# A chunked attention with two MoE layers: 64x64 score and value products, the first unit's products among them, and the third pair's operands built in place

## The chip, the cores and the metric

One core of a Trainium2 chip runs the program in one launch. The metric is device time in microseconds (us). An execution is about 2 us longer than the span of its profile, which goes from the first to the last instruction. Engines are called as in the profile: PE (matrix products), PEld (their weight loads), DVE (vector), ACT (scalar), POOL (GpSimd), SP (the queue that issues DMAs).

## What is computed

```python
def _attn_ref(q, k, v):                      # 4 batches, 8 heads, 576 x 64, chunks of 64
    scores = scale * np.matmul(q_c, k_c.transpose(0, 1, 2, 4, 3))
    scores = scores - np.max(scores, axis=-1, keepdims=True)
    attn = np.exp(scores)
    attn = attn / (np.sum(attn, axis=-1, keepdims=True) + 1e-09)
    out = np.matmul(attn, v_c)

def _moe_ref(x, w_in, w_out, s, b):          # 2304 tokens, 512 -> 2048 -> 512
    h = x @ w_in
    r = np.maximum(h, 0.0)
    g = s * (r * r) + b
    return g @ w_out

def _moe2_ref(x, w_gate, w1, w2):            # 8 experts, 512 -> 1024 -> 512
    P = np.exp(logits - logits.max())        # logits = x @ w_gate
    for _ in range(8):
        P /= P.sum(1, keepdims=True) + 1e-09
        P /= P.sum(0, keepdims=True) + 1e-09
        P *= N / E
    for e in range(E):
        out += P[:, e:e + 1] * (np.maximum(x @ w1[e], 0.0) @ w2[e])
```

Attention runs inside chunks of 64 tokens: for each chunk and head a 64x64 score matrix and a 64x64 by 64x64 value product. Its output, transposed, is the x of the first MoE layer, and that layer's output the x of the second.

## The kernel before

**Attention** goes over 18 tiles of 128 tokens (two chunks each, 8 heads in 4 pairs). `attn_stages(t)` is a generator of five stages: 0 transposes q and k on PE (`pq`, `pk`) and evicts them by ACT; 1 the scores (`sc`) with row maximum and subtraction on DVE; 2 exponential (ACT), sums and reciprocals (DVE), scaling (POOL); 3 the transpose of the probabilities (`pa`); 4 the value product (`px`), whose eviction makes the high part `xTh` (ACT) and the low part `xTl` (DVE). Both products run over all 128 partitions with zeros beside the blocks: k is evicted into the block-diagonal `kbd` (lines 259 to 263), v is loaded into the block-diagonal `vbd` (line 131), and both tiles are filled with zeros at the start (lines 888 to 891). `attention()` sets the order of the stages of the tiles, one tile entering per round.

**The first MoE layer** takes every fp32 product as three products of high and low parts (`three`, line 107). Its 2048 hidden columns are eight units of 256. For each unit `u` and each group `g` of three tiles there is `up1` (two banks `ph` of 12 products each, then relu, square, scale and the split into `gh`, `gl`) and `down1` (four banks `po` of 6). In the main loop `down1` of a group is called after `up1` of the next one (`prev`). In unit 0 the attention stages are called between the products by `stage`. The weights come as 64-bit numbers and are converted by `convert` and `finish` on ACT, DVE and POOL; `next(cg)` takes one step of that.

**The second MoE layer** multiplies 2x2 blocks by Winograd's variant of Strassen's scheme: three pairs of groups, `build_x(p)` makes the seven operands of pair `p` from the blocks a11, a12, a21, a22, each as a high part (ACT, line 519) and a low part (DVE, line 520), with sums (DVE, line 523) into scratch tiles. `up_chain(n, p)` is a chain of seven products of six matmuls; its banks come from a cycle, its evictions are `s11`, `s12` (line 665), `s22` (line 669), `s21` (674 to 677). Lines 686, 688 and 691 are copies by ACT that the chain's own later products need. `order` lists the chains; `advance` takes steps of the generators in `work` between products (preparing weight blocks `prep_w1`, building x). `prep_w1(n + 2)` is started when weight block `n` has had its last use. `prep_w2_first` makes the first operands of the down chains (line 714 the split's high part, 715 the low part, 718 the subtraction). Each `down_chain` takes four banks from `kept["abc"]`, the fourth being the target of its second product.

What sets the order on each engine is the order in which the code calls these generators: every engine works through its own instructions in program order and waits on semaphores.

## Time and profile before

| | before |
|---|---|
| median of 3 runs | 1969.03 us (1967.58 to 1971.49) |
| the profiled execution | 1969.52 us, span 1967.7 us |
| PE / PEld | busy 98% / 97% of the span |
| DVE / ACT / POOL | busy 70% / 50% / 8% |
| DMA queue 1 | 333.5 MB, 52.2% of 16 engines' span |
| granted PE clock, mean | 0.996 |

The span divides into attention with unit 0 (to 150 us), units 1 to 7 of the first layer (to about 519 us), the up chains of the second layer (to about 1235 us) and its down chains. A busy PE is not a PE at its peak, since matmuls are pipelined and their ends are modelled; durations of one matmul overlap those of the next, so spacing is read from one row's start to the next row's start. `x16` in a row of the timeline means sixteen instructions merged; a number in brackets is the idle time ahead of it and what ended that.

### The profile page before, as it was taken

What the parts mean: (1) busy time and instruction counts of PE and PEld (TensorE: products, weight loads), DVE (VectorE), ACT (ScalarE), POOL (GpSimd) and SP (SyncE); (2) the same over time, 40 slices, a digit from 0 to 9 for tenths busy, and PEclk for the clock granted to TensorE, in tenths of its full rate; (3) what the DMA queues carried; (4) which work ended last, traced back from release to release, by engine and by line L of the source; (5) the groups of instructions that cost most, each with busy time, mean ns of one, the idle gap of its engine ahead of it and who ended that gap; (6) DMA issues with size and microseconds to landing.
All of it is one profiled execution on the core that took longest, in us unless ns stands there. A gap on an engine that the chain in (4) does not pass through costs nothing.

```text
span 1967.7 us, 33548 instructions
## 1 busy us (share of the span) xinstructions
PE 1933.7 (98%) x13283; PEld 1911.3 (97%) x13283; DVE 1374.4 (70%) x2365; ACT 993.6 (50%) x1793; POOL 158.1 (8%) x128
## 2 busy tenths in 40 slices
PE   7999999999899999999999999999999999999999
PEld 6899999999799999999999999999999999999998
DVE  5656777775767666656565656888887878788775
ACT  5664333335544445444444444555555555555553
POOL 4333333330000000000000000000000000000000
PEclk9999999999999999999999999999999999999999
DMA  8521111100155565556555656867676766767675
GB/s 201 133 65 44 44 43 43 43 22 11 39 201 213 196 228 219 208 202 227 218 210 202 225 218 232 287 184 225 177 229 188 223 201 208 220 190 227 180 228 167
DMA packets 295726, 335.64 MB, mean 171 GB/s; under 512 B 65937, under 2 KB 254353, under 8 KB 295569
## 3 DMA queue, kind: packets, MB, share of 16 engines
q1 hardware_dynamic: 295568, 333.50, 52.2%
q8 instruction: 104, 1.70, 0.3%
q14 instruction: 54, 0.43, 0.1%
HBM read 196.63 MB, written 136.84 MB: 169 GB/s over the span
## 4 chain that ended last, share of the span: by engine, by line
PE 92%; ACT 3%; DVE 3%; issue 1%; POOL 0%; DMA 0%; SPq 0%; DVEq 0%; ACTq 0%; POOLq 0%
PE wb L611 71%; PE po L107 10%; PE ph L107 9%; PE px L303 1%; PE sc L272 1%; ACT kbd L261 0%; ACT whole L659 0%; PE pa L295 0%; DVE x L520 0%; ACT r L368 0%; DMA raw<-in_moe_w_in_dram 0%; ACT r L358 0%; DVE sm L287 0%; DVE xs L523 0%; ACT qT L254 0%
## 5 line engine op out<-in xcount | busy, mean ns | idle before, releaser
L611 PE MATMUL wb<-x,x 128*128 128x256 f32 x6048 | 727.2, 283 | 2.3 <-DVE whole L665 1.4
L611 PEld LDWEIGHTS wb<-x,x 128*128 128x128 f32 x6048 | 726.3, 192 | 3.2 <-DVE whole L665 1.6
L611 PE MATMUL wb<-x,w1h 128*128 128x384 f32 x2688 | 687.8, 337 | 6.9 <-ACT wb L686 3.2
L611 PEld LDWEIGHTS wb<-x,w1h 128*128 128x128 f32 x2688 | 485.5, 188 | 9.8 <-ACT wb L686 4.2
L611 PE MATMUL wb<-x,w1l 128*128 128x384 f32 x1344 | 452.3, 337 | 0.1
L816 DVE TENSOR_TENSOR x<-st,x 128x1024 fp32r<-128x1024 f32 (+1 forms) x288 | 308.0, 1088 | 101.5 <-ACT x L815 100.5
L815 ACT ACTIVATE x<-st 128x1024 fp32r<-128x1024 f32 (+1 forms) x288 | 272.1, 945 | 109.6 <-issue 74.4
L611 PEld LDWEIGHTS wb<-x,w1l 128*128 128x128 f32 x1344 | 253.2, 188 | 0.4 <-DVE w1l L573 0.4
L843 DVE SCALAR_TENSOR_TENSOR whole<-wb,lg,whole 128x256 f32<-128x256 f32 (+1 forms) x333 | 165.9, 529 | 49.7 <-PE wb L611 47.2
L849 ACT ACTIVATE wb<-wb 128x256 f32<-128x256 f32 x216 | 79.4, 368 | 232.3 <-PE wb L611 221.7
L674 DVE SCALAR_TENSOR_TENSOR whole<-wb,whole 128x384 f32<-128x384 f32 x192 | 98.0, 552 | 126.9 <-PE wb L611 105.5
L659 ACT ACTIVATE whole<-whole 128x384 f32<-128x384 f32 x192 | 100.3, 527 | 157.1 <-DVE whole L665 119.4
L107 PE MATMUL po<-gh,wh 128*128 128x384 f32 x384 | 130.1, 339 | 0.0
L107 PE MATMUL ph<-xTh,wh 128*128 128x384 f32 x384 | 129.0, 336 | 0.7 <-ACT xTh L311 0.7
L107 PE MATMUL ph<-xTl,wh 128*128 128x384 f32 x384 | 128.4, 334 | 0.3 <-DVE xTl L312 0.3
L107 PE MATMUL po<-gh,wl 128*128 128x384 f32 x384 | 128.4, 334 | 0.0
L107 PE MATMUL po<-gl,wh 128*128 128x384 f32 x384 | 128.4, 334 | 0.0
L107 PE MATMUL ph<-xTh,wl 128*128 128x384 f32 x384 | 128.3, 334 | 0.0
L360 DVE SCALAR_TENSOR_TENSOR r<-r,s_bc 128x384 f32<-128x384 f32 x84 | 65.9, 785 | 70.7 <-ACT r L358 70.7
L573 DVE TENSOR_TENSOR w1l<-w,w1h 128x512 fp32r<-128x512 f32 (+1 forms) x128 | 78.9, 619 | 34.3 <-ACT w1h L571 34.3
L691 ACT ACTIVATE whole<-wb 128x384 f32<-128x384 f32 x96 | 47.4, 494 | 93.9 <-PE wb L611 93.8
L364 ACT ACTIVATE gh<-r,b_bc 128x384 fp32r<-128x384 f32 x84 | 51.8, 617 | 84.3 <-DVE r L360 84.3
(135 smaller groups left out, 2022.9 us busy)
## 6 DMA issues: line engine op xcount, KB each, us to landing
h<-whole SPq DMA_DIRECT2D x96, 1344.0 KB, 5.0
st<-h SPq DMA_DIRECT2D x216, 512.0 KB, 4.2
w<-in_moe_w_dram SPq DMA_DIRECT2D x60, 512.0 KB, 6.8
st<-h SPq DMA_DIRECT2D x72, 256.0 KB, 4.2
raw<-in_moe_w_in_dram SPq DMA_DIRECT2D x16, 512.0 KB, 3.7
raw<-in_moe_w_out_dram SPq DMA_DIRECT2D x14, 512.0 KB, 3.5
vbd<-in_v_dram SPq DMA_DIRECT2D x72, 64.0 KB, 2.5
out_dram<-whole SPq DMA_DIRECT2D x18, 256.0 KB, 3.3
```

Source lines behind the costliest of these rows:

```text
L107: nc.tensor.matmul(out, lhsT=x, rhs=y, start=(i == 0), stop=(i == n - 1))
L360: nc.vector.scalar_tensor_tensor(out=r, in0=r, scalar=s_bc[:, 0:1], in1=r, op0=ALU.mult, op1=ALU.mult)
L364: nc.scalar.activation(out=hh, in_=r, func=AF.Identity, bias=b_bc[:, 0:1])
L573: nc.vector.tensor_tensor(out=dst(lo), in0=src, in1=dst(hi).bitcast(F32), op=ALU.subtract)
L611: nc.tensor.matmul(out, lhsT=x, rhs=y, start=fresh and i == 0, stop=i == n - 1, skip_group_check=True)
L659: nc.scalar.activation(out=dst, in_=src, func=AF.Relu)
L674: nc.vector.scalar_tensor_tensor(out=dst, in0=view(b), scalar=0.0, in1=y, op0=ALU.max, op1=op)
L691: nc.scalar.activation(out=u2, in_=b, func=AF.Copy)
L815: nc.scalar.activation(out=h, in_=src, func=AF.Copy)
L816: nc.vector.tensor_tensor(out=l, in0=src, in1=h.bitcast(F32), op=ALU.subtract)
L843: nc.vector.scalar_tensor_tensor(out=dst, in0=src, scalar=g, in1=dst, op0=ALU.mult, op1=ALU.add)
L849: nc.scalar.activation(out=dst, in_=src, func=AF.Copy)
```

## The change

The diff has six parts.

1. **Scores and values on 64x64 blocks.** `kbd` and `vbd` go, with their zero fills. k is evicted whole into `kT` by one activation. Each head and chunk has its own product with 64 rows and 64 columns of the array; a tile's scores lie in two banks and its values in two, and the row maximum, the subtraction and the two evictions of the values are done per bank. For the second chunk the two heads of a pair change places (`head`). v is loaded three tiles ahead instead of two.
2. **First loads.** q and k of tile 1 and v of tile 0 are issued ahead of the first weight block; the conversions begin at later stages.
3. **Unit 0.** `down1` of a group follows `up1` of the same group, with attention stages dealt between the products by a list.
4. **The third pair's operands** are built in place, in another order, at listed places of the first chains; the chains (0, 2) and (1, 1) change places, and the logits of the last group are made in the first chain.
5. **`prep_w2_first`** makes operand 2 ahead of operand 1.
6. **The down chains' fourth bank** is 7 and 6 in place of 6 and 7.

```diff
@@ attention
-    kbd = [cv.tile([P, NP, 2, 2, CH], F32, ...), ...]
-    vbd = [cv.tile([P, NP, 2, 2, D], F32, name=f"vbd{i}") for i in range(2)]
+    vs = [cv.tile([P, NP, 2, D], F32, name=f"vs{i}") for i in range(3)]
+    def head(s, c):
+        return s if c == 0 else 1 - s
...
-        for j in range(2):
-            h = slice(j * D, (j + 1) * D)
-            nc.scalar.activation(
-                out=kb[h, :, :, j, :],
-                in_=pk[h].rearrange("x (p c t) -> x p c t", p=NP, c=2), func=AF.Copy,
-            )
+        kT = at.tile([P, NP, P], F32, tag="kT", name=f"kT{t}")
+        nc.scalar.activation(out=kT.rearrange("x p t -> x (p t)"), in_=pk, func=AF.Copy)
...
+        sc = [bank(f"sc{t}_{s}")[:, :NP * CH] for s in range(2)]
         for p in range(NP):
-            for c in range(2):
-                nc.tensor.matmul(
-                    sc[c * CH:(c + 1) * CH, p * P:(p + 1) * P],
-                    lhsT=qT[:, p, c * CH:(c + 1) * CH],
-                    rhs=kb[:, p, c].rearrange("x j t -> x (j t)"),
+            for s in range(2):
+                for c in range(2):
+                    h = slice(head(s, c) * D, (head(s, c) + 1) * D)
+                    k = slice(c * CH, (c + 1) * CH)
+                    nc.tensor.matmul(
+                        sc[s][k, p * CH:(p + 1) * CH], lhsT=qT[h, p, k], rhs=kT[h, p, k],
...
+        for s in range(2):
+            sc3 = sc[s].rearrange("t (p k) -> t p k", p=NP)
+            nc.vector.tensor_reduce(out=mx[:, s], in_=sc3, axis=AX.X, op=ALU.max)
+            nc.vector.tensor_tensor(
+                out=pr[:, s::2], in0=sc3, in1=mx[:, s].to_broadcast([P, NP, CH]), op=ALU.subtract)
...
+        px = [bank(f"px{t}_{c}")[:, :NP * CH] for c in range(2)]
         for p in range(NP):
             for c in range(2):
+                for s in range(2):
+                    r = slice(s * CH, (s + 1) * CH)
+                    nc.tensor.matmul(
+                        px[c][head(s, c) * D:(head(s, c) + 1) * D, p * CH:(p + 1) * CH],
+                        lhsT=vb[r, p, c, :], rhs=aT[r, p, c * CH:(c + 1) * CH],
@@ build_x, third pair only
+        if p == NPR - 1:
+            split(0, a11)
+            yield
+            split(6, a22)
+            combine(a22, a21, a22, ALU.add)
+            yield
+            split(1, a22)
+            combine(a21, a21, a11, ALU.subtract)
+            yield
+            combine(a11, a22, a11, ALU.subtract)
+            split(2, a11)
+            yield
+            split(3, a12)
+            combine(a12, a12, a11, ALU.subtract)
+            yield
+            split(4, a12)
+            yield
+            split(5, a21)
+            yield
+            return
@@ down_banks, prep_w2_first
-        kept["abc"] = itertools.cycle([(0, 2, 5, 6), (1, 3, 4, 7)])
+        kept["abc"] = itertools.cycle([(0, 2, 5, 7), (1, 3, 4, 6)])
...
-            w2_split(0, 1, b22, f)
-            yield
             w2_split(0, 2, b11, f)
             w2_combine(b21, b21, b11)
+            yield
+            w2_split(0, 1, b22, f)
@@ main loop, unit 0
-            if i in (0,2,4,7,10,13,16,18):
+            if i in (4, 7, 8, 10, 11, 13):
                 next(cg, None)
...
+                if u == 0:
+                    steps = iter((2, 1, 0, 2, 2, 2, 2, 1))
+                    def side():
+                        stage(next(steps, 2))
+                        if g == 0:
+                            next(cg, None)
+                hs = up1(u, g, side)
+                if u == 0 and g < NG - 1:
+                    stage(next(steps))
+                    later()
+                    stage(next(steps))
+                    down1(u, g, hs, side)
...
@@ up chains
-        order = [(0, 0), (0, 1), (1, 0), (1, 1), (0, 2), (1, 2)] + ...
+        order = [(0, 0), (0, 1), (1, 0), (0, 2), (1, 1), (1, 2)] + ...
-        work += [prep_w1(1), build_x(2), next_weights(2)]
+        work += [prep_w1(1), next_weights(2)]
+        third = build_x(2)
...
-                advance(3 if i == 5 else 2 if i == 0 or left in (4, 5) else 1)
+                if (i, s) in ((0, 3), (1, 0), (1, 2), (2, 0), (2, 1), (2, 3), (3, 0)):
+                    next(third)
+                if i == 0:
+                    for _ in range((2, 1, 9, 0)[s]):
+                        next(lgen, None)
+                advance(2 if i == 5 or left in (4, 5) else 1)
```

Three places show what moves. On SP's queue, the first loads of the program; before:

```order
L120 DMA q_112<-in_q_dram 128x8x64
L120 DMA k_113<-in_k_dram 128x8x64
L177 DMA raw_156<-in_moe_w_in_dram 128x4x256
L120 DMA whole<-in_q_dram 128x8x64
L120 DMA whole<-in_k_dram 128x8x64
L177 DMA raw_160<-in_moe_w_in_dram 128x4x256
L131 DMA vbd_110<-in_v_dram 64x4x64 x4
```

and after:

```order
L118 DMA q_111<-in_q_dram 128x8x64
L118 DMA k_112<-in_k_dram 128x8x64
L118 DMA q_113<-in_q_dram 128x8x64
L118 DMA k_114<-in_k_dram 128x8x64
L129 DMA vs_108<-in_v_dram 64x4x64 x4
L118 DMA whole<-in_q_dram 128x8x64
L118 DMA whole<-in_k_dram 128x8x64
L175 DMA raw_162<-in_moe_w_in_dram 128x4x256
```

The first weight block (`raw`) has moved behind q and k of tiles 1 and 2 and v of tile 0.

On PE, behind the second bank of up products of group 0; before, three rounds of attention follow and then group 1's `ph`:

```order
L107 MATMUL ph_0_1_533<-xTh_192,wl_155 128x384
L295 MATMUL pa_553<-ident,pr 128x128 x4
L252 MATMUL pq_560<-ident,whole 128x128 x4
L258 MATMUL pk_567<-ident,whole 128x128 x4
L272 MATMUL sc_582<-kbd,qT_504 64x128 x8
L295 MATMUL pa_606<-ident,whole 128x128 x4
L303 MATMUL px_613<-aT_558,vbd_111 128x64 x8
L252 MATMUL pq_628<-ident,whole 128x128 x4
```

and after, where `sc_0` and `sc_1` are the two banks of one tile (two of four such pairs of rows are shown):

```order
L269 MATMUL sc_0_634<-kT_535,qT_528 64x64 x2
L269 MATMUL sc_1_635<-kT_535,qT_528 64x64 x2
L292 MATMUL pa_661<-ident,pr_115 128x128 x4
L249 MATMUL pq_668<-ident,q_113 128x128 x4
L255 MATMUL pk_675<-ident,k_114 128x128 x4
L105 MATMUL po_0_0_684<-gh_0_0_552,wh_152 128x384
L105 MATMUL po_0_0_684<-gl_0_0_553,wh_152 128x384
L105 MATMUL po_0_0_684<-gh_0_0_552,wl_153 128x384
L105 MATMUL po_0_0_684<-gh_0_1_621,wh_152 128x384
L105 MATMUL po_0_0_684<-gl_0_1_622,wh_152 128x384
```

Group 0's down products (`po_0_0`) now stand four short steps behind its `ph`; before they stood behind the `ph` of group 1.

On DVE, between the last evictions of chain 0 (`s21`) and the first of chain 1 (`s12`, `s22`); before, where `xs` are the scratch sums and `x_1` the low parts of the third pair:

```order
L674 SCALAR_TENSOR_TENSOR whole<-wb_5306,whole 128x3x128 x2
L676 TENSOR_TENSOR whole<-whole 128x3x128
L677 TENSOR_TENSOR whole<-whole 128x3x128
L523 TENSOR_TENSOR xs_2_5381<-xs_2_5380,whole 128x768
L520 TENSOR_TENSOR x_1_5296<-xs_2_5380,x_0_5295 128x768
L523 TENSOR_TENSOR xs_2_5421<-whole,xs_2_5381 128x768
L520 TENSOR_TENSOR x_1_5296<-xs_2_5381,x_0_5295 128x768
L665 TENSOR_TENSOR whole<-wb_5310,whole 128x3x128
L669 TENSOR_TENSOR whole<-wb_5307,c_0_1_5373 128x3x128
```

and after:

```order
L694 SCALAR_TENSOR_TENSOR whole<-wb_5700,whole 128x3x128 x2
L696 TENSOR_TENSOR whole<-whole 128x3x128
L697 TENSOR_TENSOR whole<-whole 128x3x128
L593 TENSOR_TENSOR w1l_5723<-w_1_5660,w1h_5722 128x2x2x128
L519 TENSOR_TENSOR x_1_5690<-whole,x_0_5689 128x768
L522 TENSOR_TENSOR whole<-whole 128x768
L685 TENSOR_TENSOR whole<-wb_5704,whole 128x3x128
L689 TENSOR_TENSOR whole<-wb_5701,c_0_1_5777 128x3x128
```

Two of the four operations of the third pair have moved away from here, and one low part of weight block 1 has come.

## Rows read from the trace of the kernel before

**Rows 1.** Stretches: length, busy us of each engine, PEclk, DMA share, GB/s.
```profile
0.00:35.27 35.27, 23.35 (x172) 19.57 (x173) 19.43 (x36) 19.86 (x34) 18.25 (x26) 0.90 0.84 195
35.27:150.45 115.18, 110.65 (x888) 103.93 (x886) 69.83 (x130) 75.97 (x143) 36.31 (x31) 0.97 0.46 110
63.12:91.18 28.06, 27.77 (x249) 25.60 (x249) 19.26 (x37) 20.41 (x39) 9.51 (x8) 1.00 0.52 117
150.45:470.00 319.55, 319.55 (x1845) 319.55 (x1845) 221.58 (x392) 129.13 (x240) 103.54 (x72) 1.00 0.12 39
...
1220.00:1225.00 5.00, 5.00 (x22) 5.00 (x21) 3.65 (x8) 1.81 (x4) 0.00 (x0) 0.66 0.48 191
```

**Rows 2.** Timeline of PE, start: start us, duration us, instruction, idle ahead.
```profile
8.06 1.12 PE L252 MATMUL pq<-ident,whole 128*128 128x128 f32 x4 [1.84 <-DMA whole<-in_q_dram]
...
18.55 1.09 PE L295 MATMUL pa<-ident,pr 128*128 128x128 f32 x4 [2.83 <-POOL pr L290]
...
35.30 0.42 PE L107 MATMUL ph<-xTh,wh 128*128 128x384 f32 x1
```

**Rows 3.** Timeline of PE, one attention round at full clock, and group 0's logits.
```profile
79.25 0.34 PE L107 MATMUL po<-gh,wl 128*128 128x384 f32 x1
79.52 1.09 PE L272 MATMUL sc<-kbd,qT 128*64 128x128 f32 x16
80.54 0.66 PE L295 MATMUL pa<-ident,pr 128*128 128x128 f32 x4
81.03 1.90 PE L303 MATMUL px<-aT,vbd 128*128 128x64 f32 x16
82.74 0.42 PE L107 MATMUL po<-gh,wh 128*128 128x384 f32 x1
...
83.87 0.60 PE L252 MATMUL pq<-ident,whole 128*128 128x128 f32 x4
84.31 0.60 PE L258 MATMUL pk<-ident,whole 128*128 128x128 f32 x4
...
470.86 0.85 PE L409 MATMUL pl<-whole,wg 128*32 128x384 f32 x8
```

**Rows 4.** Groups by line, ACT, 35.27 to 150.45: busy us, mean ns, idle ahead.
```profile
L261 ACT ACTIVATE kbd<-pk 64x512 f32<-64x512 f32 x28 | 16.5, 588 | 0.3
...
L311 ACT ACTIVATE xTh<-px 128x512 fp32r<-128x512 f32 x15 | 8.9, 594 | 4.8 <-PE px L303 4.7
```

**Rows 5.** The page's costliest groups: an ACT copy of 128x256.
```profile
L849 ACT ACTIVATE wb<-wb 128x256 f32<-128x256 f32 x216 | 79.4, 368 | 232.3 <-PE wb L611 221.7
```

**Rows 6.** Timeline of DVE: one operation at 512 and at 256 columns.
```profile
573.91 0.68 DVE L573 TENSOR_TENSOR w1l<-w,w1h 128x512 fp32r<-128x512 f32 x1
...
576.55 0.42 DVE L573 TENSOR_TENSOR w1l<-w,w1h 128x256 fp32r<-128x256 f32 x1
```

**Rows 7.** Timeline of PE, first up product of group 1.
```profile
63.12 0.44 PE L107 MATMUL ph<-xTh,wh 128*128 128x384 f32 x1 [0.69 <-ACT xTh L311]
```

**Rows 8.** Timeline of ACT, first bank of group 0: relu and high part.
```profile
37.74 0.49 ACT L358 ACTIVATE r<-ph 128x384 f32<-128x384 f32 x1
...
38.91 0.62 ACT L364 ACTIVATE gh<-r,b_bc 128x384 fp32r<-128x384 f32 x1 [0.69 <-DVE r L360]
```

**Rows 9.** Waits of PE, 505 to 610: us in total, times, longest.
```profile
PE wb L611 <- ACT w1h L571: 2.2, 1, 2.2
...
PE wb L611 <- DVE whole L669: 1.4, 1, 1.4
PE wb L611 <- ACT wb L686: 1.1, 1, 1.1
```

**Rows 10.** Waits of PE, 1185 to 1260.
```profile
PE wb L611 <- ACT wb L686: 2.2, 2, 1.8
PE wb L611 <- DVE whole L665: 1.4, 1, 1.4
```

**Rows 11.** Timeline of ACT before the down chains: a split of `prep_w2_first`.
```profile
1218.38 0.63 ACT L714 ACTIVATE x<-whole 128x512 fp32r<-128x512 f32 x1 [1.49 <-DVE whole L718]
```

More of the change, by code (lines that the diff above doesn't have):

```diff
@@ L129, in load_v @@
             bb, s0 = divmod(t * P + c * CH, S)
-            for j in range(2):
+            for h in range(2):
                 nc.sync.dma_start(
-                    out=vbd[t % 2][j * CH:(j + 1) * CH, :, c, j, :],
+                    out=vs[t % 3][h * CH:(h + 1) * CH, :, c, :],
                     in_=v[bb, :, s0:s0 + CH, :].rearrange(
                         "(p two) s d -> two s p d", two=2
-                    )[j],
+                    )[head(h, c)],
                 )
@@ L245, in attn_stages @@
             xT[g] = new_x(g)
-        vb = vbd[t % 2]
-        kb = kbd[t % 2]
+        vb = vs[t % 3]
         a = qt.pop(t)
@@ L887, in chunk_attention_ffn_moe @@
         nc.gpsimd.memset(ones, 1.0)
-        for z in kbd:
-            nc.vector.memset(z, 0.0)
-        for z in vbd:
-            nc.gpsimd.memset(z, 0.0)
         plan_unit(0)
-        load_raw(0)
         load_qk(1)
-        load_raw(1)
         load_v(0)
         load_qk(2)
+        load_raw(0)
+        load_v(1)
+        load_raw(1)
+        load_v(2)
         load_raw(2)
         load_raw(3)
-        load_v(1)
         nc.sync.dma_start(out=s_bc, in_=s.partition_broadcast(P))
@@ L956, in chunk_attention_ffn_moe @@
                     next(cg, None)
-                hs = up1(u, g, side if u else lambda: stage(3))
-                if u == 0 and g == 0:
-                    for _ in cg:
-                        pass
-                    plan_unit(1)
-                    cg = unit_conversion(4)
-                    next(cg)
-                elif u == 0 or g:
+                if u == 0:
[10 more added lines that the diff above has]
+                    down1(u, g, hs, side)
+                    if g == 0:
+                        for _ in cg:
+                            pass
+                        plan_unit(1)
+                        cg = unit_conversion(4)
+                    else:
+                        next(cg, None)
+                    continue
+                if u == 0 or g:
                     next(cg, None)
@@ L1020, in advance @@
                         work.pop(0)
-        order = [(0, 0), (0, 1), (1, 0), (1, 1), (0, 2), (1, 2)] + [(n, p) for n in range(2, NF - 2) for p in range(NPR)]
+        order = [(0, 0), (0, 1), (1, 0), (0, 2), (1, 1), (1, 2)] + [(n, p) for n in range(2, NF - 2) for p in range(NPR)]
         order += [(NF - d, p) for d, p in ((2, 1), (2, 0), (1, 1), (2, 2), (1, 0), (1, 2))]
```

49 lines of the change are left out of this document (17 added, 32 removed).

## The prediction

> **What bounds the kernel now.** I read the profile from the outside in: busy time by stage, then TensorE's own waits, then the rows of the engines that it waited for. By stage [rows 1], PE is busy for all 319.55 us between 150.45 and 470 us, and for 23.35 of the first 35.27, 110.65 of the next 115.18; behind 470 us its waits sum to some microseconds, in the first chains of the second MoE and at the change to the down chains [rows 9, 10]. So the time is PE's work plus a few waits in three places, and an edit counts only where it shortens PE's row of work or one of those waits. The diff touches just these three places; the rest of the program keeps its instructions. No other engine is near full: in the densest part of the attention stage (63 to 91 us) DVE is busy 19.26 of 28.06 us and ACT 20.41 [rows 1].
>
> All sums are made against the profiled execution, 1969.52 us; it is 0.5 us above the median of the three runs, which is less than any step below is certain.
>
> **Attention, start (to 35.30, the first product of unit 0).** PE waits here for transfers and for tile 0's softmax: for q of tile 1 until 8.06, for POOL's scaling of tile 0 until 18.55 [rows 2]. Ahead of tile 1's q and k in SP's queue stood a weight block of 512 KB, which at the 195 GB/s of this stretch [rows 1] is 2.7 us. The new order puts q and k of tile 1 first, and the conversions of the weight blocks start four stages later, so ACT and DVE do tile 0 first. The weight blocks are then late by the transfers that pass them: for the first block q, k of tiles 1 and 2 and v of tile 0, 1.3 MB or 6.6 us; ph of group 0 needs two of them converted by then, so the cover is there but no longer wide. I take 4 us earlier; bounds 1 and 6. The removed zero fills ran while PE waited for the first q: nothing. The bursts of this stretch lie beside waits: nothing.
>
> **Attention, the products.** Count the tiles behind 35.3: kbd has 28 evictions there, so 14 tiles' scores; xTh has 15, so 15 tiles' values [rows 4]. One sc burst takes 1.02 us from its start to the next instruction (79.52 to 80.54), and the product ahead of it is followed after 0.27 instead of the usual 0.173 (319.55 us over 1845 products), so entering this array mode costs 0.10: 1.12 in all. One px burst takes 1.71 (81.03 to 82.74) [rows 1, 3]. A pass of 128 columns over the whole array takes 0.11 (four transposes in 0.44, 83.87 to 84.31). Sixteen sc passes of the same width would be 1.76 in a row; they take 1.02, since the two halves of the array work side by side: 8 x 0.109 = 0.87, and 0.15 for leaving. The logits row says so more strongly: eight passes of 384 columns on four strips of the array in 0.85, where one after the other is 8 x 0.33 = 2.6 [rows 3]. px has only 64 columns a pass but 128 of weights, and costs 0.107 a pass.
>
> After the change both bursts are 32 passes of 64 columns with 64 columns of weights, eight on each quarter of the array. A pass is then about half of 0.109, 0.055. If the four quarters run side by side a burst is 8 x 0.055 + 0.25 = 0.69: sc saves 0.43 x 14 = 6.0, px 1.02 x 15 = 15.3, together **21.3 us**. Other ends: quarters in pairs only, 16 x 0.055 + 0.25 = 1.13, sc nothing, px 0.58 x 15 = 8.7; no overlap, 32 x 0.055 + 0.25 = 2.01, a loss of 12.5 + 4.5 = 17.0. Before shows column strips side by side, and no quarter that shares its columns with another; I take the four, since halves and strips both kept their full rate.
>
> The Trainium skill, TensorEngine Tiling (Array Packing), Restrictions and Gotchas, speaks against it: row tiles write to different PSUM banks and cannot access one bank at the same time. Here each bank receives quarters of both row halves (on different partitions). By that rule a burst is the pair price. No run here shows two row tiles.
>
> ACT saves one eviction per tile (two kbd of 0.588 become one kT) and splits xTh (0.594) into two of about 0.37, the 128x256 row [rows 4, 5]; DVE's three operations per tile become halves, each 0.42 against 0.68 for the whole [rows 6], 0.16 more for a pair. All of it lies beside PE as long as neither engine fills up (third rival).
>
> **Attention, new waits.** Before, down products ran one group behind; now po of a group follows its own ph. Two places get less cover. First, px now stands directly ahead of ph of groups 1 to 3, where PE needs the evicted values. Once this happened before, at 63.12, and cost 0.69 and a little more for the low part [rows 7]; with two ACT halves in a row I take three waits of 1.5, less the one there was: 3.5 us. Second, the chain ph, r, r squared, gh, gl: r starts at 37.74, gh ends at 39.53 [rows 8], and gl adds 0.6, so 2.4 us behind ph. PE has pa, one burst, pq, pk and the five po products that come before gl is needed: 0.44 + 0.69 + 0.88 + 0.87 = 2.9 in groups 0 to 3, two px (1.4 + 0.87) in group 4. Alone that would cover it; ACT and DVE also serve the softmax, and in group 0 the last weight conversion (DVE, ACT, POOL in turn) ends there too. I take 3 us. Bounds for both together: 0 and 12.
>
> Sum to the first product of unit 1: before 150.45; 264 unit-0 products stand ahead of it in both programs, so their cost cancels. 4 + 21.3 - 6.5 = **18.8 us** earlier.
>
> **First chains of the second MoE.** PE waits 1.4 us there for DVE L669, 1.1 for ACT L686 and 2.2 for ACT's w1h [rows 9]. The first two come from the third pair's build: four DVE operations of about 0.9 stand between two chain evictions. Now two of these and a 0.6 split stand there, some 1.1 less of 1.4, and ACT's queue has one split (0.83) less ahead of L686. The 2.2 goes because chain (0, 2) moves up one place: the last use of weight block 0 is one chain (42 x 0.173 = 7.3 us) earlier, and with it the preparation of block 2. What could come late instead is the third pair itself, needed one chain sooner; its last splits are placed one product ahead of use. The logits of group 5 move from a later chain into the first, at the same price. I take **4 us**, bounds 1 and 5.
>
> **Change to the down chains.** PE waited 1.8 us for ACT L686 (of 2.2 in two) [rows 10], and ACT had itself been held 1.49 by a split that waited for DVE's subtraction L718 [rows 11]. The swap of the splits puts one there whose operand is long done. Behind that wait the granted clock fell to 0.66 over 5 us, the mean of 1.2 and 2.4 GHz stretches [rows 1], 1.7 us lost; without the wait I expect no fall. Against it: the moved split returns one step later with DVE full. The other wait, 1.4 for DVE L665 [rows 10], is for the bank that the first down chain takes as its fourth; it now takes one that nothing holds. But that chain's third product needs a copy that ACT makes behind the same L665, so I give it 0.3. Together **3.5 us**, bounds 0 and 5.
>
> **Total**: 18.8 + 4 + 3.5 = 26.3, 1969.5 - 26.3 = **1943 us**.
>
> **The rivals.**
> *Slower: quarters don't overlap.* The products then do more passes for the same work. For it: no trace row has two row tiles at once. Against it: strips and halves overlap. The bursts lose 17.0, the start and the two later places still give 4 + 4 + 3.5, and the new waits vanish behind a busier PE: 5.5 us slower, 1975. It is even where a burst takes 1.82 us: 29 bursts x 1.82 is 52.8, what the bursts cost now (14 x 1.12 + 15 x 1.71 = 41.3) plus 11.5.
> *Pairs only.* 8.7 in place of 21.3, 12.6 less: 1956. By the rule on PSUM banks above this is what comes.
> *Evictions bound.* DVE would have 69.83 [rows 1] + 15 x 3 x 0.16 = 77.0 us of work behind 35.3. If it can't be held busier than in its densest stretch (19.26 of 28.06, 69%), that takes 112 us in place of 115.18: 3 + 4 + 7.5 = 14.5 in all, 1955. For it: the halves need two PSUM banks where one did, and eight are shared. Against it: in that stretch PE, not DVE, set the pace. The skill's same page, Performance Considerations (PSUM Bottleneck), warns of just this, that tiling speeds up TensorE but not the evacuation.
>
> **How the numbers follow.** Forecast 0.52 (1931 to 1950), pairs 0.20, evictions 0.14, no overlap 0.10, and 0.04 that stalls in the stage eat everything. The low end: 6 + 21.3 - 0 + 5 + 5 = 37.3, 1932; with a little for a kinder clock in the first stage (0.97 there [rows 1]) 1930. The high end takes in pairs and evictions with 5 us more of waits: 1961. Above lie the 0.10 and a part of the 0.04, below some 0.05. A measurement of this kernel tells about 0.2% (4 us) from no change. Faster 0.85, same 0.04, slower 0.11.
>
> **What would show it.** Right: sc and px bursts near 0.6 to 0.7 us, four passes starting together; unit 1's first product near 132 us; no PE wait for w1h in the first chains; no fall of the clock near the down chains. Wrong: bursts of 1.1 (pairs) or 2.0 (none); PE waits behind px and ph far above 6 us in sum, with DVE or ACT above 75% of the stage; a new wait for the third pair's splits in chain (0, 2). If the first product of unit 0 doesn't come before 33 us, the step on the load order is wrong.

## The result and the profile after

The changed kernel takes 1985.02 us (median of four runs) against 1968.64 for the kernel before: a ratio of 1.008, 95% interval 1.0062 to 1.0097. It is 16 us slower, where 1943 was forecast. Its profiled run took 1984.83 us, span 1983.0.

The stretches of the changed kernel that answer to the first two of [rows 1], cut at its own first products of unit 0 (37.81, in [rows 2] 35.30) and of unit 1 (166.18, before 150.45):

```profile
0.00:37.81 37.81, 21.40 (x284) 16.79 (x285) 19.58 (x45) 18.24 (x34) 16.85 (x24) 0.78 0.87 189
37.81:166.18 128.37, 102.43 (x1351) 87.26 (x1350) 71.74 (x170) 66.70 (x141) 35.67 (x30) 0.87 0.42 98
```

The second stretch, from unit 0's to unit 1's first product, is called the stage below. PE's busy time in it fell from 110.6 to 102.4 us, though 26.4 of these ran at half clock (before 6.8). Counting half-clock time as half, that is some 89 us of work, before 107: the 18 us that the smaller products save are there. They are outweighed: PE idles 25.9 us of the stage (before 4.5), and the granted clock is at 1.2 GHz for 34.4 us of it (before 6.8). DVE and ACT are busy for a smaller share of the stage than before, 56% and 52% (before 61% and 66%).

The timeline of PE, one round (start, duration, instruction; what it waited for), for [rows 3]:

```profile
73.51 0.69 PE L269 MATMUL sc<-kT,qT 64*64 64x64 f32 x32
74.13 0.45 PE L105 MATMUL ph<-xTh,wh 128*128 128x384 f32 x1
...
76.88 0.69 PE L302 MATMUL px<-aT,vs 64*64 64x64 f32 x32
77.50 0.66 PE L249 MATMUL pq<-ident,whole 128*128 128x128 f32 x4
78.00 0.60 PE L255 MATMUL pk<-ident,whole 128*128 128x128 f32 x4
78.35 0.42 PE L105 MATMUL po<-gh,wh 128*128 128x384 f32 x1
79.90 0.45 PE L105 MATMUL po<-gl,wh 128*128 128x384 f32 x1 [1.12 <-DVE gl L338]
```

Both bursts take 0.62 us from start to next start. Taken singly, the 32 products of the px burst start in fours: 0.02 us from the first to the fourth, and each four 0.058 us behind the one before. The waits of PE from 35 to 178 us (sum, times, longest), where before had 4.5 us idle in the whole stage, the 0.69 of [rows 7] among them:

```profile
PE po L105 <- DVE gl L338: 10.4, 6, 2.9
PE px L302 <- ACT aT L294: 4.2, 1, 4.2
PE po L105 <- ACT wh L211: 4.0, 1, 4.0
PE ph L105 <- DVE xTl L311: 2.5, 3, 1.7
PE ph L105 <- ACT xTh L310: 2.3, 3, 0.8
PE pq L249 <- ACT qT L251: 2.1, 2, 1.4
```

Behind unit 1's start the lag of 15.7 us grows by 1.8 (a last wait for gl, 1.47 of it, at 172.66), shrinks by 0.7 in the first chains of the second MoE and by 1.4 at the change to the down chains, and ends at 15.4.

### The profile page after: what moved, and what is told of

Its sections match the earlier page's. It is cut to its first block, busy times and chain, and to the rows that moved or that the text cites. A ratio compares the mean times of both kernels' runs of the same rounds, so it can differ in the third digit from the quotient of the medians.

```text
span 1983.0 us, 34734 instructions
## 1 busy us (share of the span) xinstructions
PE 1922.5 (97%) x13859; PEld 1890.0 (95%) x13859; DVE 1379.3 (70%) x2417; ACT 983.5 (50%) x1793; POOL 156.2 (8%) x126
## 4 chain that ended last, share of the span: by engine, by line
PE 90%; DVE 5%; ACT 3%; DMA 1%; issue 1%; SPq 0%; POOL 0%; DVEq 0%; ACTq 0%
PE wb L631 69%; PE po L105 10%; PE ph L105 9%; DMA raw<-in_moe_w_out_dram 0%; DVE x L519 0%; DVE r L359 0%; DMA st<-h 0%; DVE sm L284 0%; DVE mx L277 0%; DMA raw<-in_moe_w_in_dram 0%; PE sc L269 0%; ACT r L357 0%; ACT r L367 0%; PE px L302 0%; ACT whole L679 0%
## 5 line engine op out<-in xcount | busy, mean ns | idle before, releaser
L835 ACT ACTIVATE x<-st 128x1024 fp32r<-128x1024 f32 (+1 forms) x288 | 272.1, 945 | 112.5 <-issue 79.7
L863 DVE SCALAR_TENSOR_TENSOR whole<-wb,lg,whole 128x256 f32<-128x256 f32 (+1 forms) x333 | 166.0, 530 | 49.4 <-PE wb L631 46.9
L105 PE MATMUL po<-gl,wh 128*128 128x384 f32 x384 | 132.5, 345 | 10.4 <-DVE gl L338 10.4
L105 PE MATMUL po<-gh,wh 128*128 128x384 f32 x384 | 134.2, 349 | 4.3 <-ACT wh L211 4.0
L105 PE MATMUL ph<-xTh,wl 128*128 128x384 f32 x384 | 128.4, 334 | 0.0
L711 ACT ACTIVATE whole<-wb 128x384 f32<-128x384 f32 x96 | 47.4, 494 | 91.0 <-PE wb L631 91.0
```

Of the source, the lines that this page charges most:

```text
L105: nc.tensor.matmul(out, lhsT=x, rhs=y, start=(i == 0), stop=(i == n - 1))
L711: nc.scalar.activation(out=u2, in_=b, func=AF.Copy)
L835: nc.scalar.activation(out=h, in_=src, func=AF.Copy)
L863: nc.vector.scalar_tensor_tensor(out=dst, in0=src, scalar=g, in1=dst, op0=ALU.mult, op1=ALU.add)
```

## The experiments

The theories at the start: **order** (part 3, second products right behind a group's first ones, makes PE wait and drops its clock), **attention** (the 64x64 products themselves leave PE idle), **load** (part 2 delays unit 0). In the table, time is the median and the ratio is to runs of the kernel before taken beside it; the medians of those lay between 1968.6 and 1973.1 us, so ratios compare better than times (e13 to e15 above all). The other columns are from the profiled run, in us: the first products of unit 0 and unit 1, and for the stage between them PE's busy time, *idle*, the stage's length less that, and *half*, the time at 1.2 GHz (in e3 1.6 us of it are read from products that follow each other after 0.32 us). "Last tile" is the end of the 18th tile's px; of the 18 tiles 15 lie in the stage.

| kernel | time, us | ratio, 95% interval | unit 0 | unit 1 | PE busy | idle | half | last tile |
|---|---|---|---|---|---|---|---|---|
| before | 1968.6 | | 35.3 | 150.5 | 110.6 | 4.5 | 6.8 | 129.7 |
| changed | 1985.0 | 1.008 (1.0062-1.0097) | 37.8 | 166.2 | 102.4 | 25.9 | 34.4 | 154.0 |
| e1 attention only | 1964.4 | 0.9967 (0.9954-0.9980) | 35.1 | 145.4 | 95.4 | 14.9 | 13.7 | 124.6 |
| e2 order only | 1997.1 | 1.0131 (1.0116-1.0146) | 35.1 | 175.0 | 118.1 | 21.8 | 23.9 | 161.9 |
| e3 changed, old order | 1964.1 | 0.9966 (0.9953-0.9979) | 37.8 | 147.3 | 94.1 | 15.4 | 11.9 | 126.5 |
| e4 second MoE only | 1966.4 | 0.9981 (0.9972-0.9991) | 34.1 | 149.1 | 110.4 | 4.6 | 6.8 | 128.4 |
| e5 attention, second MoE | 1961.9 | 0.9958 (0.9944-0.9973) | 34.3 | 145.8 | 96.6 | 15.0 | 17.1 | 125.0 |
| e6 e1 without maximum | 1953.0 | 0.9913 (0.9898-0.9928) | 34.7 | 131.9 | 89.9 | 7.3 | 6.8 | 111.0 |
| e7 changed, gl first | 1983.5 | 1.0071 (1.0056-1.0086) | 38.0 | 166.0 | 102.6 | 25.5 | 34.3 | 153.7 |
| e8 e1, wide evictions | 1964.1 | 0.9967 (0.9956-0.9979) | 33.4 | 142.2 | 93.9 | 14.8 | 13.7 | 120.9 |
| e9 changed without maximum | 1971.1 | 1.0003 (0.9993-1.0013) | 37.9 | 152.8 | 98.5 | 16.5 | 24.3 | 140.8 |
| e10 changed, more stages | 1981.6 | 1.0055 (1.0035-1.0075) | 37.3 | 162.1 | 98.7 | 26.0 | 30.7 | 123.0 |
| e11 e5, r and gl off DVE | 1958.5 | 0.9935 (0.9918-0.9951) | 34.8 | 141.2 | 90.7 | 15.6 | 3.4 | 120.4 |
| e12 before without maximum | 1963.5 | 0.9964 (0.9953-0.9975) | 36.6 | 144.4 | 106.8 | 1.0 | 0.5 | 123.7 |
| e13 changed, filler | 1982.6 | 1.0057 (1.0038-1.0076) | 37.2 | 164.9 | 110.9 | 16.9 | 17.1 | 151.8 |
| e14 e5, r off DVE | 1958.6 | 0.9936 (0.9921-0.9951) | 33.5 | 142.7 | 94.9 | 14.4 | 13.7 | 121.9 |
| e15 e11, wide evictions | 1956.5 | 0.9924 (0.9907-0.9941) | 35.3 | 141.2 | 91.9 | 14.0 | 10.2 | 120.3 |

**e1: part 1 alone.** The kernel before with `kT`, `vs` and the 64x64 products; v's third tile is loaded behind the others.

```diff
         load_v(1)
+        load_v(2)
```

> The kernel before with the 64x64 attention alone (kT, vs, the sc and px products, no clearing of tiles of zeros); loads, conversions, unit 0's order and the second MoE are those of before. Order theory (the loss comes from unit 0's second products standing right behind its first ones, and TensorE then waits for gl, aT and xTl and drops its clock): the burst saving of about 18 us of busy time at full clock stays in, first product of unit 1 near 130 to 138 us, time 1948 to 1956 us. Attention theory (shorter bursts leave TensorE idle between stages and the clock falls, whatever the order): unit 1 starts at 150 us or later, half-clock time of the stage above 20 us, time 1967 to 1985 us.

1964.4 us: 5 us faster, between the two theories. Neither is right as it stood: the attention does gain, but the stage is only 4.9 us shorter where PE's busy time fell by 15.2 (95.4 for 110.6 us). The rest reappears as idle time, 14.9 for 4.5 us. The rounds of this run (a group's first product to the next one's), busy PE, PEld, DVE, ACT, POOL:

```profile
35.12:62.35 27.23, 20.07 (x331) 16.13 (x329) 16.95 (x46) 15.12 (x33) 9.77 (x9) 0.87 0.89 198
62.35:89.30 26.95, 24.14 (x393) 20.96 (x393) 20.04 (x52) 17.46 (x38) 10.01 (x9) 0.94 0.59 131
89.30:116.03 26.73, 21.78 (x389) 18.77 (x385) 21.12 (x55) 17.03 (x39) 9.22 (x8) 0.99 0.39 92
```

Before, the second such round was 28.1 us with PE full [rows 1]. Now it is 26.95 with 2.8 us of PE idle and DVE at 74%, in the third round 79%. The chain of waits of this run (what the end was waiting for, followed back; start, duration) lies on DVE for 59% of this round and of the third, where before it lay on PE for 91% of the round of [rows 1]. A piece of it, pauses under 0.1 us left out:

```profile
85.59 0.64 ACT whole L282
86.32 0.70 DVE sm L284
87.04 0.18 DVE sm L285
87.25 0.20 DVE sm L286
87.45 0.30 DVE mx L277
87.78 0.42 DVE pr L278
88.20 0.34 DVE mx L277
88.57 0.42 DVE pr L278
88.99 0.34 DVE xTl L311
```

So a third theory, **VectorE**: with the smaller products the row of evictions and softmax steps on DVE paces the rounds. e6 and e12 test it.

**e2: part 3 alone,** in the kernel before. It holds for groups 0 to 3, since this kernel keeps attention tiles where group 4's sums go; the line that differs from the changed kernel's:

```diff
-                if u == 0 and g < NG - 1:
+                if u == 0 and g < NG - 2:
```

> The kernel before with only the new order of unit 0 (second products right behind the first for groups 0 to 3; groups 4 and 5 as before, since before's placement keeps attention tiles where group 4's sums go), block-diagonal attention. Order theory: slower than before, waits po<-gl and half-clock time as in the changed kernel, some 10 to 30 us, time 1978 to 2000 us. Attention theory: within 4 us of before, 1965 to 1973 us.

1997.1 us, as the order theory has it; the attention theory's 1965 to 1973 is out. The longest waits of PE in this run:

```profile
PE po L107 <- DVE gl L339: 9.5, 4, 4.2
PE ph L107 <- ACT xTh L311: 4.8, 4, 2.7
PE po L107 <- ACT wh L213: 3.8, 1, 3.8
```

Unit 1 starts 24.5 us later than before, with the block-diagonal attention. The price is the order's own.

**e3: the changed kernel with unit 0 in the old order.**

```diff
-                hs = up1(u, g, side)
-                if u == 0 and g < NG - 1:
-                    stage(next(steps))
-                    later()
-                    stage(next(steps))
-                    down1(u, g, hs, side)
...
+                hs = up1(u, g, side if u else lambda: stage(3))
```

> The changed kernel with unit 0 in the order of before (second products of a group behind the first ones of the next, three stages between chains); loads, conversion places and the second MoE as changed. Order theory: 1945 to 1958 us, unit 1's first product near 130 to 138 us. Attention theory: 1975 to 1987 us. Load theory (the later raw blocks and conversions delay unit 0): start of unit 0 at 37 to 38 us as in the changed kernel, and 5 to 10 us slower than the run with the attention alone.

1964.1 us: 21 us of the changed kernel's loss are gone, but the 1945 to 1958 of the order theory isn't reached, for e1's reason. Unit 0 starts at 37.8 in this run and in the changed kernel, at 35.1 and 34.3 in the two with the old loads that are nearest (e1, e5): part 2 costs some 2.5 to 3.5 us at the start instead of giving 4. Over all runs of the table the start lies at 37.2 to 38.0 with the new loads and at 33.4 to 36.6 with the old ones. The load theory has the sign, but not the price: in place of 5 to 10 us over e1, the time is e1's, and 2 over e5, which shares parts 4 to 6. The stage, 109.5 us, is about as long as e1's. This pair, e3 and the changed kernel, differs in part 3 alone: of the 18.8 us by which the stage is longer in the changed kernel, 10.5 are idle time of PE, and 8.3 are longer busy time for the same products, of which 8.0 go back to the clock (26.4 busy us at half clock against 10.5).

**e4: parts 4 to 6 alone,** in the kernel before.

> The kernel before with only the changes in the second MoE: the third pair's sums in place, in their new places, the new order of the first chains, and the changed banks and split of the down transition. By the drift between the two traces (0.6 us gained in the first chains, 1.4 us at the transition): 1966 to 1968 us, about 2 us faster than before. If the first chains' gain is real once unit 0 isn't disturbed (my forecast): 1960 to 1963 us. If it costs: above 1970 us.

1966.4 us. In the profile the first chains gain 0.6 us and the transition 2.1, so 2.7 us in place of 7.5 (the time itself is 3.4 us below the median of the kernel before beside it).

**e5: parts 1 and 4 to 6,** with loads and unit 0's order as before.

> The 64x64 attention together with the changes in the second MoE, with loads, conversion places and unit 0's order as before. If the two parts add up (drift of the traces: 5.05 us for the attention, 2.5 us for the second MoE; times: 5.4 and 3.4 us): 1961 to 1963 us. If the second MoE takes the attention's gain back, as the waits for w1l in the changed kernel suggest: 1964 us or more.

1961.9 us: the two add up.

**e6: e1 without the row maximum.**

```diff
-            sc3 = sc[s].rearrange("t (p k) -> t p k", p=NP)
-            nc.vector.tensor_reduce(out=mx[:, s], in_=sc3, axis=AX.X, op=ALU.max)
-            nc.vector.tensor_tensor(
-                out=pr[:, s::2], in0=sc3, in1=mx[:, s].to_broadcast([P, NP, CH]), op=ALU.subtract)
+            nc.scalar.activation(
+                out=pr[:, s::2], in_=sc[s].rearrange("t (p k) -> t p k", p=NP),
+                func=AF.Exp, scale=1.0 / float(D) ** 0.5)
...
-        nc.scalar.activation(out=pr, in_=pr, func=AF.Exp, scale=1.0 / float(D) ** 0.5)
```

> The run with the 64x64 attention alone, less the row maximum and its subtraction: exp reads the scores from PSUM (two passes of ScalarE for one), so VectorE loses 4 operations of a tile (2 of 0.395 us, 2 of 0.424 us, 1.64 us of a tile, some 16 us in the rounds of unit 0). The softmax's value is the same up to rounding; what is left out is the shift. VectorE theory (with the 64x64 bursts VectorE's row of evictions and softmax steps paces the rounds of 27 us): rounds of 23.5 to 25.5 us, 1956 to 1960 us. Order or TensorE theory (the rounds are TensorE's own work, waits and clock): 1962 to 1966 us, like the attention alone.

1953.0 us, better than the VectorE theory's range. DVE lost 18.3 us of the stage (73.98 to 55.69), the stage 13.1:

```profile
34.73:131.89 97.16, 89.87 (x1351) 80.73 (x1350) 55.69 (x118) 66.81 (x157) 37.95 (x31) 0.96 0.58 134
```

In a round of it (60 to 85 us) the chain of waits lies on PE again, for 89%. The forecast gain of the bursts exists once these steps on DVE are out of the way. That unit 1 starts at 131.9, where I had forecast 132 for the changed kernel, is chance: this run has neither the start's 4 us nor the new waits of my sum, and it leaves out softmax steps that the changed kernel has. This run is no replacement: without the shift, large scores could overflow.

**e7: the changed kernel with gl ahead.**

```diff
                 if u == 0 and g < NG - 1:
+                    later()
                     stage(next(steps))
-                    later()
                     stage(next(steps))
```

> The changed kernel with the last gl of a chain issued ahead of the two attention stages that stand between a group's first and second products, where it stood behind the first of them. If the po<-gl waits (10.4 us, 6 of them) are the cost of the new order: they fall to under 3 us, and with the clock time behind them the kernel is 10 to 15 us faster than the changed one, 1970 to 1975 us. If the cost is that the attention runs two groups later beside fewer products (its last tile ends at 154 us for 130 us before), the waits move elsewhere: within 4 us of the changed kernel, 1981 to 1987 us.

1983.5 us, within 4 us of the changed kernel: the gl waits stay at 10.4 us in 6. PE waits for the first gl of a group, not the last, and that one stands behind the softmax. DVE in the changed kernel:

```profile
99.57 0.69 DVE L284 TENSOR_REDUCE sm<-whole 128x8 f32<-128x512 f32 x1 [2.18 <-ACT whole L282]
...
101.37 0.41 DVE L277 TENSOR_REDUCE mx<-sc 128x4 f32<-128x256 f32 x1
101.81 0.42 DVE L278 TENSOR_TENSOR pr<-sc,mx 128x256 f32<-128x256 f32 x1
102.16 0.61 DVE L359 SCALAR_TENSOR_TENSOR r<-r,s_bc 128x384 f32<-128x384 f32 x1
102.68 0.61 DVE L338 SCALAR_TENSOR_TENSOR gl<-r,b_bc,gh 128x384 fp32r<-128x384 f32 x1
```

PE, with ph long done, gets one product in and waits:

```profile
99.97 0.44 PE L105 MATMUL po<-gh,wh 128*128 128x384 f32 x1 [0.24 <-ACT r L357]
103.35 0.69 PE L105 MATMUL po<-gl,wh 128*128 128x384 f32 x1 [2.94 <-DVE gl L338]
```

**e8: e1 with a pair of banks read as one operand.**

```diff
+        scd = pd.tile([P, 2, 512], F32, tag="pd", name=f"sc{t}")
+        sc = [scd[:, s, :NP * CH] for s in range(2)]
...
+        nc.vector.tensor_reduce(out=mx, in_=sc3, axis=AX.X, op=ALU.max)
```

> The 64x64 attention alone, with each pair of PSUM banks of the scores and of px read as one operand: one operation of 512 columns in the place of two of 256 for the maximum, the subtraction, xTh and xTl (VectorE 0.638+0.691+0.686 for 0.790+0.848+0.830 us of a tile, 0.45 us less). While unit 0 runs the banks are 4 single ones and 2 pairs for 8 single ones. VectorE theory: 5.4 us less of VectorE work over 12 tiles, rounds 0.5 to 1.0 us shorter, 1960 to 1963 us. If banks are the limit (fewer single ones): slower than the attention alone, 1965 to 1972 us. If neither: 1964 us.

1964.1 us, e1's time. (The tiles are 18, not 12: the operations would save 6.8 us in the stage; DVE's busy time falls by 3.2.) PE waits 6.7 us in sum for sc's banks instead of 3.7 in e1, and 3.3 instead of 0.3 for px's, so the fewer banks may have taken back what the wide reads gave. Inconclusive.

**e9: the changed kernel without the row maximum** (e6's edit).

> The changed kernel, less the row maximum and its subtraction (exp reads the scores from PSUM; the shift of the softmax is left out, its value stays but for rounding). VectorE theory, as it held with unit 0 in the old order (15 us of VectorE work gone moved unit 1's start by 13.5 us): unit 1 starts at 150 to 154 us for 166.2, time 1968 to 1973 us. Order theory (in the new order TensorE stands in its own queue before products whose operands are just being made, VectorE is busy for only 57% of the stage): the chain of a tile is 1.6 us shorter, so 3 to 8 us, time 1977 to 1982 us.

1971.1 us; unit 1 at 152.8, 13.4 us earlier, the same as in the old order (13.5). My reading that DVE at 56% can't bind was wrong here too: its steps are links of a serial round, not a full queue. And the order's price stays: the stage is 17.8 us longer than e6's (unit 1 starts at 152.8 against 131.9, of which 3 us are there at unit 0's start already, with the new loads).

**e10: the changed kernel with more stages beside the chains.**

```diff
-                    steps = iter((2, 1, 0, 2, 2, 2, 2, 1))
+                    steps = iter((3, 3, 3, 3, 3, 3, 3, 3))
```

> The changed kernel with three attention stages at each of the eight places of a group in unit 0, for the changed kernel's 2, 1, 0, 2, 2, 2, 2, 1. If the new order loses because too few stages stand beside each chain, so that the attention ends late (154 us for 130 us): it ends 10 us or more earlier, 1968 to 1976 us. If it loses because second products stand right behind their own first ones, whatever the number of stages: 1980 to 1990 us.

1981.6 us. The attention ends at 123.0, 31 us earlier, and unit 1 starts only 4 us earlier: position, not the number of stages. What is left behind the attention, some six chains of 24 products or 4.16 us each, takes 39 us. Group 3, with no attention near it, PE:

```profile
132.69 0.34 PE L105 MATMUL ph<-xTh,wl 128*128 128x384 f32 x1
134.59 0.45 PE L105 MATMUL po<-gh,wh 128*128 128x384 f32 x1 [1.56 <-ACT gh L363]
137.16 0.69 PE L105 MATMUL po<-gl,wh 128*128 128x384 f32 x1 [2.12 <-DVE gl L338]
137.64 0.52 PE L105 MATMUL po<-gh,wl 128*128 128x384 f32 x1
137.96 0.52 PE L105 MATMUL po<-gh,wh 128*128 128x384 f32 x1
```

Between a group's first and second products there is nothing for PE to do; it waits 3.7 us and goes on at 0.32 us a product, where 0.17 was usual ahead of it. (1.0 of the 3.7 is gl's own: it takes 1.62 us in place of 0.61, beside a POOL operation that runs from 135.09 to 136.68.) In e1 the five chains behind the attention take 20.90 us, and PE is busy for all of it.

**e11: e5 with r on ScalarE and gl on GpSimd in unit 0.**

```diff
-            if u < NU1 - 1:
+            if 0 < u < NU1 - 1:
...
-                nc.vector.tensor_tensor(out=hl, in0=r, in1=hh.bitcast(F32), op=ALU.subtract)
+                eng.tensor_tensor(out=hl, in0=r, in1=hh.bitcast(F32), op=ALU.subtract)
```

> The 64x64 attention with the changes in the second MoE, unit 0 in the old order, and in unit 0 alone r made by ScalarE (Square, then Identity with scale and bias, as the last unit has it) and gl by GpSimd. By the rows of the units behind, VectorE loses 0.65 to 0.75 us (r) and 0.61 us (gl) for each of 12 chains, some 15 us, of which 9 to 10 us in the rounds; ScalarE gains 1.1 us a chain. VectorE theory: unit 1 starts 5 to 9 us earlier, 1953 to 1957 us. Otherwise (ScalarE takes its place, or TensorE): 1960 to 1963 us, as without it.

1958.5 us, 3.4 better than e5, somewhat less than expected. DVE has 17.3 us less, nearly as much less as in e6, but the stage is 5.1 us shorter where e6's was 13.1: the rounds are 26 us still. ACT is busy for 79.6 us (66.5 in e5), POOL for 48.7 (37.3), and PE now waits 5.6 us for POOL's scaling, where a gl of 1.01 us stands ahead of it. Over two rounds the chain of waits lies on DVE for 31%, on ACT for 29% and on POOL for 13%. So what paces the rounds isn't DVE's total alone, but the row of steps through DVE, ACT and POOL; e6 took four steps out of that row as well as work off DVE, and no run here separates the two.

**e12: the kernel before without the row maximum.**

> The kernel before, less the row maximum and its subtraction (exp reads the scores from PSUM; the shift of the softmax is left out). If TensorE bounds its rounds, as I read rows of before (27.8 us busy of 28.1 us at full clock): no more than 4 us faster, 1965 to 1970 us. If VectorE paces the rounds in before too: unit 1 starts 8 to 14 us earlier, 1955 to 1961 us.

1963.5 us; the stage is 7.3 us shorter, between the two bounds.

```profile
36.63:144.44 107.81, 106.84 (x887) 101.28 (x885) 52.84 (x102) 73.72 (x140) 35.19 (x29) 1.00 0.49 117
```

PE is full here at full clock, so its own work, 107 us, was before's bound to within these 7 us, which came as 3.5 us of idle time and 3.2 of half clock. Taking the row maximum and its subtraction off DVE alone gives 7.3 us of the stage (e12), relieving PE alone 4.9 (e1), both 18.0 (e6).

**e13: filler products in the waits.**

```diff
+            if u == 0 and g < NG - 1 and d == 0:
+                for _ in range(16):
+                    nc.tensor.matmul(po, lhsT=units[0][0][0][:, 0, 0:P], rhs=xT[g][0][:, 0],
+                                     start=True, stop=True)
```

> The changed kernel with 16 products of 384 columns more (unit 0's weights and inputs once again, into the bank that the first sum overwrites) ahead of the second products of groups 0 to 4, where TensorE waits for gh and gl: 2.8 us of a group at full clock, some 14 us in all, of which the waits hide about 10. Clock theory (the waits cost above all by the half clock behind them): half-clock time of the stage falls from 34.4 us to under 12 us, and 5 to 12 us are gained in spite of the filler, 1972 to 1980 us. Wait theory (the waits themselves and the attention's steps that stand behind them): no gain, 1983 to 1992 us.

1982.6 us, between the two ranges and nearer to the waits; the intervals of its ratio and the changed kernel's overlap. The gl waits fell to 1.6 us and the half clock to 17.1, yet the stage is only 0.7 us shorter:

```profile
37.22:164.93 127.71, 110.85 (x1432) 97.54 (x1430) 71.61 (x170) 66.73 (x141) 35.78 (x31) 0.93 0.43 99
```

Filler of 13.8 us (80 x 0.173) displaced 9.1 us of idle time, and the shorter half clock gave back some 5.4 (PE is busy for 110.9 us, not 102.4 + 13.8). The two together pay for the filler and no more: the clock theory's gain isn't there, and the serial round keeps its length. That the clock is the smaller part of the order's price is what e3 shows, with 8.0 us of 18.8.

**e14: e11 with gl back on VectorE.**

```diff
-            lows.append((r, hh, hl, 0 < u < NU1 - 1, nc.vector if u else nc.gpsimd))
+            lows.append((r, hh, hl, 0 < u < NU1 - 1, nc.vector))
```

> The 64x64 attention with the changes in the second MoE and unit 0 in the old order; in unit 0 r is made by ScalarE, and gl stays on VectorE (a subtraction of 0.555 us for the three-operand form of 0.61 us). If GpSimd's queue held the run with gl on GpSimd (pr behind a gl of 1.01 us): as fast or faster than it, 1955 to 1958 us. If VectorE's work decides (6.7 us of gl back on it): 1959 to 1962 us.

1958.6 us, between the two ranges and the same as e11 within the intervals: moving r off DVE gives the gain, and what gl's place adds these runs don't tell (unit 1 starts at 141.2 in e11, at 142.7 here).

**e15: e11 with e8's wide evictions.**

> The run with r on ScalarE and gl on GpSimd, with pairs of PSUM banks read as one operand as well (one eviction of 512 columns for two of 256; 4 single banks and 2 pairs while unit 0 runs). VectorE theory: 5.4 us of it less, of which what the other engines don't take back, 1954 to 1957 us. If the fewer banks cost what the wide reads give, as with the attention alone: 1957 to 1961 us.

1956.5 us, the fastest that keeps the reference's softmax: 0.9924 of before, some 28 us under the changed kernel. Its interval overlaps e11's and e14's.

## Why the prediction was wrong

**What bounds the kernel: half right.** PE's work bounded the stage, but "no other engine is near full" was read from a share. DVE at 69% in the densest stretch [rows 1] was part of the next bound, right behind PE: its steps, with some of ACT's, stand in a row between PE's, and PE's work could shrink by 18 us but the stage by 4.9 (e1). This is the step that failed for the attention: "All of it lies beside PE as long as neither engine fills up." DVE's work in e1 came out at 74.0 us, below the 77.0 of the third rival, and neither DVE nor ACT was full.

**Bursts: right mechanism, nearly the size, lost gain.** The 0.69 forecast held 0.10 for entering the array mode. The 0.62 doesn't: the transposes ahead of the burst at 73.51 are followed after 0.53 us instead of 0.44, so a burst costs some 0.71. PE's work fell by 18 us for 21.3. The quarters do run side by side, as the starts in fours show. The rule of the Trainium skill (TensorEngine Tiling (Array Packing), Restrictions and Gotchas) that different row tiles can't access one PSUM bank at once would have given 1.13; here both row halves wrote one bank, on different partitions, at 0.62, and the measurement decides. But of these 18 us e1 kept 4.9 in the stage: 10.4 went into idle time and 3 into half clock. The rival "evictions bound" was the nearest to this, at 1955 with 0.14: its own term, 3 us off the stage, came out as 4.9, and the kernel without the order took 1964 because the terms for the start and the second MoE failed as well. The Trainium skill's warning beside it (the same page, Performance Considerations, PSUM Bottleneck), that tiling speeds up TensorE but not the evacuation of PSUM, agrees with e1, where 4.9 of 18 us reached the stage.

**New waits: the miss that turned the sign.** 6.5 us, bounds 0 to 12; the order costs 24.5 at unit 1's start in e2, 18.9 between e3 and the changed kernel, and 17.8 of the stage between e6 and e9. The half for px ahead of ph was right: PE waits 4.8 us there in sum, 4.5 forecast. The half for gl failed: 3 us forecast, 10.4 in six waits, with 4.0 more for a weight block's conversion (3.8 in e2). I compared the PE work that covers gl with an empty DVE (2.9 against 2.4 us), and counted it up to the fifth po product, which needs the second bank's gl. The second product already needs the first bank's gl, and the program has DVE make that one behind the second bank's r. In the run both stand behind a softmax [e7's rows], PE waits in its own queue, and so do the attention's next products behind it: from the sixth tile to the 18th it takes 86 us (67.6 to 154.0) against 63 in e1 (61.6 to 124.6). Where the attention is hurried instead (e10), the bare hand-over of each group is exposed. Of the 18.8 us, 10.5 are idle time and 8.0 the clock (e3); which of PE's waits come from the hand-over itself and which from the slowed attention isn't settled. The sign that I had named for such waits, DVE or ACT above 75% of the stage, didn't come: they are at 56% and 52%.

**Start: wrong sign.** -4 us forecast, +2.5 measured. POOL's first scaling came earlier (PE's wait ends at 14.86 for 18.55), as forecast, but the first weight block's conversion starts at 14.80 for 7.22, and the last conversions now stand among the last stages ahead of unit 0. In the changed kernel:

```profile
14.86 0.66 PE L292 MATMUL pa<-ident,pr 128*128 128x128 f32 x4 [1.23 <-POOL pr L287]
...
32.74 0.63 ACT L211 ACTIVATE wh<-m 128x512 fp32r<-128x512 f32 x1 [2.33 <-DVE m L206]
33.27 0.58 ACT L294 ACTIVATE aT<-pa 128x512 f32<-128x512 f32 x1
...
33.91 0.69 PE L302 MATMUL px<-aT,vs 64*64 64x64 f32 x32 [2.69 <-ACT aT L294]
```

ACT's `aT` waits in its queue behind a `wh` that waits for DVE's `m`. I had named this cover as thin and priced it at nothing.

**First chains: -4 forecast, some -0.6.** The w1h wait of 2.2 [rows 9] went, as forecast; what took its place, in the changed kernel:

```profile
PE wb L631 <- ACT wb L706: 2.1, 3, 1.2
...
PE wb L631 <- DVE w1l L593: 1.6, 1, 1.6
```

PE now waits for the low part w1l of a weight block, which stands in DVE's queue beside the third pair's operations, and the pair's splits still stand in ACT's queue ahead of L706. The term was mis-sized: I took away the waits that were there and let nothing take their place.

**Down transition: -3.5 forecast, -1.4 to -2.1.** The 1.8 for L686 [rows 10] and the clock's fall are gone, as forecast, but PE waits 2.3 us for L711, a copy by ACT that the chain needs (L691 before). It stood in ACT's queue behind the split L835, which waited for a transfer of the down chains' first input:

```profile
1246.68 1.06 ACT L835 ACTIVATE x<-st 128x1024 fp32r<-128x1024 f32 x1 [3.13 <-DMA st<-h]
1247.64 0.47 ACT L711 ACTIVATE whole<-wb 128x384 f32<-128x384 f32 x1
...
1248.17 0.63 PE L631 MATMUL wb<-x,w1h 128*128 128x384 f32 x2 [2.26 <-ACT whole L711]
```

All eleven kernels with parts 4 to 6 have this wait, 1.4 to 2.3 us, behind 2.3 to 3.1 us of waiting for that transfer. Before, the same split found its transfer landed. The transfer had no term in my sum.

**The sum.** The measured terms account for the result: the start +2.5, the attention -4.9 (e1), the order +18.9, the last gl +1.8, the first chains -0.7 and the transition -1.4 make +16.2 us, and the span grew by 15.3. The forecast was -26.3; of the 42 us between, some 35 lie in the attention's term (16), the new waits (12) and the start (6.5).

## What to carry to other kernels

An engine at 70% can be the next bound right behind a full one, if its steps lie in a row between another engine's: ask how long the round is when the full engine costs nothing, before booking what you save on it. In an in-order queue a consumer placed directly behind its producer exposes the whole eviction chain, and everything behind it waits too; one group of distance was worth some 18 to 25 us here. Conversions issued later don't vanish: look which queue they then stand in. A wait taken off the critical path uncovers the next one: look what stands behind it in the same queue, transfers among them.

## What the runs showed of the hardware

Operands that span two PSUM banks cost DVE no more than one bank's 512 columns: 0.640 us for the maximum and 0.691 for the subtraction in e8, 0.638 and 0.691 before.

Some of DVE's operations wait for POOL. In e1 the addition L285 on eight numbers takes 0.17 us 15 times of 18, and 0.53 to 1.23 where a POOL operation runs:

```profile
82.49 1.23 DVE L285 TENSOR_SCALAR sm<-sm 128x8 f32<-128x8 f32 x1
83.75 0.20 DVE L286 RECIPROCAL sm<-sm 128x8 f32<-128x8 f32 x1
```

```profile
82.42 1.27 POOL L199 TENSOR_TENSOR m<-l,m 128x512 f32<-128x512 f32 x1
```

It ends when POOL's does. In e10 gl, 0.61 us where POOL is idle, takes 1.62 beside a POOL operation:

```profile
150.56 1.62 DVE L338 SCALAR_TENSOR_TENSOR gl<-r,b_bc,gh 128x384 fp32r<-128x384 f32 x1
```

The Trainium skill (SBUF — State Buffer, A bandwidth-pool intuition that's wrong) has GpSimd and a two-port operation of VectorE blocking each other; the rows of L285 agree, if it is one.
